# Two all-seeing rounds of the next batch moved to the end of the attention before, in a block-sparse attention with a GELU feed-forward

## The chip, the core and the metric

The kernel runs on one core of one Trainium2 chip. The metric is the device time of one execution in microseconds (us); the time of a kernel is the median over its runs. Engines: TensorE (PE, with its weight loads PEld), VectorE (DVE), ScalarE (ACT), GpSimd (POOL) and SyncE (SP).

## What is computed

The attention is a BigBird pattern: each query block of 32 tokens sees the first and the last key block, its neighbours, itself and three sampled blocks; the first and last query block see every key (these are called all-seeing here). The result, with the heads side by side, goes through a feed-forward layer with an exact GELU.

```python
batch, n_heads, seq, head_dim = (4, 8, 768, 64)
block = 32; n_blocks = 24; n_rand = 3
scores = scale * np.matmul(q, k.transpose(0, 1, 3, 2))
mask = np.abs(blk_i - blk_j) <= 1
mask = mask | (blk_i == 0) | (blk_j == 0) | (blk_i == n_blocks - 1) | (blk_j == n_blocks - 1)
for qb in range(n_blocks):
    for kb in sampled_blocks[qb]:
        mask[qb * block:(qb + 1) * block, kb * block:(kb + 1) * block] = True
scores = np.where(mask, scores, -1000000000.0)
attn = softmax(scores)
x = (attn @ v), heads side by side           # 3072 x 512
h = x @ w_in                                 # 512 -> 2048
out = (0.5 * h * (1.0 + erf(h / sqrt(2)))) @ w_out
```

## The kernel before

**Units.** The 3072 tokens are worked off in nine units. Batch 0 has three (one, two and three quads of 128 tokens), batches 1 to 3 have two each: a *first half* (quads 0 to 2, with the two all-seeing blocks) and a *second half* (quads 3 to 5). For each unit there is an attention, an FFN1 (`ffn1_step`: eight steps of 8 matmuls and a Gelu, writing `g`) and an FFN2 (`ffn2_pieces`: 16 matmuls for each quad, 48 for three quads, 32 for two). The FFN2 of a unit is dealt out, matmul by matmul, into the attention of the unit that follows: it is the `filler`.

**Rounds.** An attention goes in rounds. An ordinary round holds up to two query blocks for all eight heads: scores on PE (`scores`, L301) into one of two PSUM buffers, the negated maxima on DVE (`maxima`, L326), exponentials on ACT (`exponentials`, L338, one instruction for each block and group of heads), a 32x32 transpose on DVE (`turned`, L355). After two rounds the values follow on PE (`values`, L403) in two halves, then a division on DVE (`divided`, L418 to L422), a transpose on PE (`outputs`, L432) and a copy on ACT into `xT` (L437), which FFN1 reads. The all-seeing blocks make four rounds ("d", x, G): x says first or last block, G the group of heads. Their maxima are L329, their transposes go into `ptd` (L359), their values are L379. A first half has these four and six ordinary rounds, a second half six ordinary ones.

**Order.** Nothing reorders the instructions: each engine runs them in the order in which the program issues them. `attention` issues, for each `it`: the scores of round it+1, a division if one is due, the transpose of round it-1, the maxima of round it+1, the exponentials of round it, a finished FFN2 output, hooks, `quota[it + 1]` matmuls of FFN2, an `xT` output, and the values due. The last iteration first takes two FFN2 matmuls. Behind the loop stand the load of ACT's table for Gelu (the one for Exp is loaded in the last step of FFN1) and the `tail`: counts of FFN2 matmuls between the last values, division and output.

**FFN2's output.** One PSUM bank (`psO`, one buffer) collects an output tile. After 16 matmuls, `store_finished` copies it on ACT into `os` (L459; three buffers) and SP stores it (L461). It is called after the exponentials of an iteration, after its FFN2 matmuls unless `late` is set, and before the first matmul of the next output.

**Keys and queries of the next batch.** They are loaded by POOL (`load_by_token`, L111, six transfers for keys and six for queries) in FFN1 of a first half, after `hold_loads(0)`, a one-element copy that waits for FFN1's first Gelu. `turn` (L117, L118) has SP transpose them by DMA into `kTd` (the same memory as `ptd`) and into `qTs`; it is a hook at `it` = 2 of the second half's attention. `place_keys` and `spare_key` (L122, L236) copy the keys, scaled, to their places on DVE; this is done in FFN1 of the second half. There DVE also gathers the keys and values of the blocks seen (`gather_fixed`, `gather`: L249 to L265).

Of the kernel before, what the change touches and what calls it, by code (L numbers as in the profile page):

```python
# [19 lines left out]
def kernel(  # L20
# [121 lines left out]
            out=w_out_sb[:, w * part:w * part + w, :],  # L142
            in_=moe_w_out[P * w * part:P * w * (part + 1)].rearrange("(ko p) f -> p ko f", p=P))

    def hold_loads(m):

        nc.gpsimd.tensor_copy(mark, g[0:1, m, 0:1])  # L147

    def ones(i):
        for hh in range(4):  # L150
# [84 lines left out]
    def spare_key(kT):  # L235
        nc.vector.tensor_copy(kT[:, NB, :], kT[:, 0, :])  # L236
# [23 lines left out]
    def gather(unit, js, at, c0=0, c1=BW, engine=None):  # L260

        src = k0 if (unit.b, c1) == (0, KC) else kvs[unit.b % 2][:, :, c0:c1]
        for j in js:
            for r in range(NR):
                (engine or nc.vector).tensor_copy(sampled(unit.place[j], r)[:, None, c0:c1],  # L265
                                                  src[:, bass.ds(at[j][r], 1), :])


    class Unit:
        def __init__(self, b, quads, dense, i0=0):  # L270
            self.b, self.quads, self.dense = b, quads, dense
            self.groups = [[j for j in range(4 * t, 4 * t + 4) if 0 < j < NB - 1] for t in quads]
            self.js = [j for grp in self.groups for j in grp]
            self.place = {j: i for i, j in enumerate(self.js, i0)}
            self.rounds = [("d", x, G) for x in (0, 1) for G in (0, 1)] if dense else []
            self.ends = {3: tuple(self.rounds)} if dense else {}
            for grp in self.groups:
                r = [("s", tuple(grp[i:i + 2])) for i in range(0, len(grp), 2)]
                self.rounds += r
                self.ends[len(self.rounds) - 1] = tuple(r)  # L280
# [12 lines left out]
    def scores(unit, rnd):  # L293
        qT, kT = qTs[unit.b % 2], keys(unit.b) if unit is not units[0] else k0
        A = psA.tile([P, 1024], F32, name="sc", tag="A")

        def product(o, G, hh, j, rhs):
            r = (hh % 2) ^ G
            rows = slice(64 * r, 64 * r + 64)
            pr = 2 * G + hh // 2  # L300
            nc.tensor.matmul(o, lhsT=qT[rows, j // 4, pr, BL * (j % 4):BL * (j % 4) + BL],  # L301
                             rhs=rhs(rows, pr), start=True, stop=True)
        if rnd[0] == "s":
            A4 = A.rearrange("p (g j c) -> p g j c", g=2, j=2)
            for i, j in enumerate(rnd[1]):
                x = unit.place[j]
                for hh in range(4):
                    for G in range(2):
                        product(A4[32 * hh:32 * hh + 32, G, i, :].rearrange(
                            "p (a c k) -> p a c k", a=2, k=BL), G, hh, j,  # L310
                            lambda rows, pr: seen_keys(x, rows, pr))
        else:
            _, x, G = rnd
            for c0, c1 in ((0, 512), (512, 768)):
                for hh in range(4):
                    product(A[32 * hh:32 * hh + 32, c0:c1], G, hh, (NB - 1) * x,
                            lambda rows, pr: kT[rows, c0 // BL:c1 // BL, BL * pr:BL * pr + BL])
        st[rnd, "A"] = A
# [137 lines left out]
    def store(n, quad, cols, op):  # L456
# [3 lines left out]
        row = units[n].b * S + quad * P  # L460
        nc.sync.dma_start(out=out[row:row + P, cols], in_=os)  # L461

    finished = []

    def ffn2_pieces(n):
# [26 lines left out]
                                 start=(m == 0), stop=(m == KOUT - 1))  # L492
            store(n, quad, cols, op)

    def attention(unit, filler, quota, tail, held=0, hooks=None, late=False):

        rounds, n, hooks = unit.rounds, len(unit.rounds), hooks or {}
        due = [(max(e + 1 + half, held), grp, half) for e, grp in sorted(unit.ends.items())
               for half in range(2)]
        weighed, given = [], []  # L500

        def fill(m):
            for _ in range(m):
                next(filler, None)

        def weigh():
            _, grp, half = due.pop(0)
            values(unit, grp, half)
            if half:
                weighed.append(grp)  # L510

        def divide():
            divided(weighed[0])
            given.append(weighed.pop(0))
        for it in range(-1, n):
            last = it + 1 == n
            if not last:
                scores(unit, rounds[it + 1])
            else:
                fill(2)  # L520
                while due and due[0][0] <= it:
                    weigh()
            ready = len(given)
            if weighed and not last:
                divide()
            if it >= 1:
                turned(rounds[it - 1])
            if weighed and last:
                divide()
            if not last:  # L530
                maxima(rounds[it + 1])
            if it >= 0:
                exponentials(rounds[it])
            store_finished()
            for f in hooks.get(it, ()):
                f()
            fill(quota[it + 1])
            if not late:
                store_finished()
            if ready:  # L540
                outputs(unit, given.pop(0))
            while not last and due and due[0][0] <= it:
                weigh()
        table(AF.Gelu)
        turned(rounds[n - 1])
        fill(tail[0])
        weigh()
        fill(tail[1])
        weigh()
        assert not due  # L550
        while given:
            outputs(unit, given.pop(0))
        divide()
        fill(tail[2])
        outputs(unit, given.pop(0))
        for _ in filler:
            pass
        store_finished()
# [26 lines left out]
    attention(units[0], iter(()), [0] * 7, (0, 0, 0), 5,  # L585
              {4: [lambda: gather(units[0], units[0].js, known, KC, BW)], 5: [second_values]})

    QUOTAS = {0: ([4, 3, 1, 1, 0], (1, 2, 1)), 1: ([6, 5, 5, 3, 3, 1, 1], (2, 2, 1))}
    for n, unit in enumerate(units):
        nxt = units[n + 1] if n + 1 < len(units) else None  # L590
        b = unit.b
        fresh = nxt is not None and nxt.b != b
        if nxt is not None and not fresh:
            gather_fixed(k0 if n == 0 else keys(b), nxt.place)
            if n == 0:
                known |= block_numbers(J0[:3], DVE)
                gather(nxt, J0[:3], known, 0, KC)
                gather(nxt, J0[:3], known, KC, BW)
            elif n == 1:
                known |= block_numbers(J1[:6], DVE)  # L600
                gather(nxt, J1[:6], known)
                gather(nxt, J1[6:7], block_numbers(J1[6:7], DVE))
            else:
                gather(nxt, J1[:6], known)
                for js in (J1[6:9], J1[9:11]):
                    gather(nxt, js, block_numbers(js, DVE))
        for s in range(KOUT // 2):
            ffn1_step(n, 2 * s)
            if s == 0:
                if n == 0:  # L610
                    hold_loads(0)
                    for h in range(H):
                        load_v(1, h)
                    nc.gpsimd.tensor_copy(kvs[0][:, :, 0:KC], k0)
                    gather(units[2], J1[7:], block_numbers(J1[7:], POOL), engine=nc.gpsimd)
                if n > 0 and not fresh and b + 1 < B:
                    hold_loads(0)
                    load_by_token(kn, k, b + 1)
                    load_by_token(qn, q, b + 1)
                if fresh and b + 2 < B:  # L620
                    hold_loads(0)
                    for h in range(H):
                        load_v(b + 2, h)
                if fresh:
                    others = block_numbers(J0[7:], DVE)
            if s == 7 and nxt is not None:
                table(AF.Exp)
            if fresh and s == 0:
                place_keys(b + 1)
                spare_key(keys(b + 1))  # L630
                gather_fixed(keys(b + 1), nxt.place)
                gather(nxt, J0[:7], known)
                gather(nxt, J0[7:], others)
        filler = ffn2_pieces(n)
        if nxt is None:
            last_output(n)
        elif n in QUOTAS:
            attention(nxt, filler, *QUOTAS[n],
                      hooks={2: [lambda: turn(1)]} if n == 1 else None)
        elif fresh:  # L640
            attention(nxt, filler, [6, 6, 4, 0, 6, 6, 4, 0, 2, 2, 1], (2, 3, 3), late=True)
        else:
            attention(nxt, filler, [8, 8, 5, 5, 6, 2, 1], (2, 3, 5),
                      hooks={2: [lambda: turn(b + 1)]} if b + 1 < B else None)


# [28 lines left out]
```

## Time and profile before

| | us |
|---|---|
| median of 3 runs (319.34 to 320.63) | 319.44 |
| the profiled execution | 320.74 |
| its span, first to last instruction | 319.0 |
| PE busy | 268.3 (84%) |
| DVE busy | 218.5 (68%) |
| ACT busy | 208.4 (65%) |
| POOL busy | 88.7 (28%) |
| from FFN1 to FFN1, the three stages with a second half's attention that is followed by another batch | 27.96, 33.35, 32.42 |
| the last second half, which no batch follows | 31.23 |
| from FFN1 to FFN1, first halves | 37.88, 37.28, 37.34 |

The stages run from the first FFN1 matmul (L451) of a unit to that of the next, as the chain of waits lists them: 56.52, 84.48, 122.36, 155.71, 192.99, 225.41, 262.75 and 293.98 us. A stage so has one FFN1 and the attention of the next unit with the FFN2 in it. The first of them has batch 0's second unit, with two quads, for its FFN1. Engine times add up over stages with different limits; which engine holds a stage is read from the waits in it.

### The profile page before, as it was taken

What the parts mean: (1) busy time and instruction counts of PE and PEld (TensorE: products, weight loads), DVE (VectorE), ACT (ScalarE), POOL (GpSimd) and SP (SyncE); (2) the same over time, 40 slices, a digit from 0 to 9 for tenths busy, and PEclk for the clock granted to TensorE, in tenths of its full rate; (3) what the DMA queues carried; (4) which work ended last, traced back from release to release, by engine and by line L of the source; (5) the groups of instructions that cost most, each with busy time, mean ns of one, the idle gap of its engine ahead of it and who ended that gap; (6) DMA issues with size and microseconds to landing.
All of it is one profiled execution on the core that took longest, in us unless ns stands there. A gap on an engine that the chain in (4) does not pass through costs nothing.

```text
span 319.0 us, 12127 instructions
## 1 busy us (share of the span) xinstructions
PE 268.3 (84%) x5240; PEld 147.7 (46%) x5240; DVE 218.5 (68%) x550; ACT 208.4 (65%) x374; POOL 88.7 (28%) x147
## 2 busy tenths in 40 slices
PE   1656877988898879997998889997998789989995
PEld 0615734744453445544553445444543446444643
DVE  6487774798698768785698768874968967673000
ACT  9665483597568775785568765785577765885621
POOL 8659757570070003920160004910000000000000
PEclk9999987799999999998999999999999999999999
DMA  7999999599499100999097101998000000010001
GB/s 110 146 115 208 207 120 31 64 151 171 117 82 52 38 4 35 107 171 189 36 87 47 36 5 37 127 180 159 36 3 35 35 4 35 1 70 4 33 35 67
DMA packets 90632, 25.43 MB, mean 80 GB/s; under 512 B 81745, under 2 KB 87634, under 8 KB 90578
## 3 DMA queue, kind: packets, MB, share of 16 engines
q0 software_dynamic: 68352, 13.64, 79.4%
q1 hardware_dynamic: 22226, 11.01, 14.7%
q8 instruction: 41, 0.67, 0.9%
q14 instruction: 13, 0.11, 0.1%
HBM read 27.26 MB, written 6.29 MB: 105 GB/s over the span
## 4 chain that ended last, share of the span: by engine, by line
PE 66%; DVE 16%; ACT 7%; DMA 5%; issue 3%; POOL 1%; DVEq 0%; POOLq 0%; ACTq 0%
PE hp L451 28%; PE op L470 18%; PE av L403 10%; DVE xh L422 5%; DVE pT L355 4%; PE sc L301 4%; ACT pp L338 4%; DMA w_in_sb<-in_moe_w_in_dram 3%; DVE nm L326 2%; DMA kv<-in_v_dram 2%; PE av L491 2%; PE op L491 2%; DVE rec L420 2%; PE av L379 2%; ACT xT L437 2%
## 5 line engine op out<-in xcount | busy, mean ns | idle before, releaser
L338 ACT ACTIVATE pp<-sc,nm 128x256 bf16<-128x256 f32 (+1 forms) x192 | 92.0, 594 | 22.0 <-DVE nm L326 17.7
L470 PE MATMUL op<-w_out_sb,g 128*128 128x512 bf16 x336 | 91.4, 387 | 2.3 <-ACT os L459 1.3
L451 PE MATMUL hp<-xT,w_in_sb 128*128 128x384 bf16 (+2 forms) x576 | 88.9, 320 | 3.7 <-ACT xT L437 3.7
L454 ACT ACTIVATE g<-hp 128x768 bf16<-128x768 f32 (+4 forms) x81 | 53.8, 676 | 39.2 <-PE hp L451 39.1
L451 PEld LDWEIGHTS <-w_in_sb 128*128 128x128 bf16 x576 | 57.1, 104 | 35.9 <-issue 6.3
L326 DVE TENSOR_REDUCE nm<-sc 128x4 f32<-128x1024 f32 (+1 forms) x48 | 53.4, 1113 | 7.9 <-PE sc L301 7.4
L265 DVE COPY gb<-kv 128x388 bf16 (+1 forms) x240 | 52.2, 295 | 6.1 <-issue 5.9
L403 PE MATMUL av<-kv,pT 64*32 64x130 bf16 x1760 | 39.9, 231 | 15.7 <-DVE xh L422 8.7
L403 PEld LDWEIGHTS <-pT 64*32 64x32 bf16 x2816 | 30.2, 95 | 39.5 <-DVE xh L422 16.4
L470 PEld LDWEIGHTS <-g 128*128 128x128 bf16 x336 | 27.8, 98 | 34.2 <-issue 12.8
L355 DVE STREAM_TRANSPOSE pT<-pp 128x512 f32<-128x512 f32 (+1 forms) x48 | 31.5, 655 | 7.3 <-ACT pp L338 6.9
L147 POOL COPY mark<-g 1x1 bf16<-1x1 bf16 x6 | 6.0, 1002 | 106.6 <-ACT g L454 106.6
L437 ACT COPY xT<-tx 128x512 bf16<-128x512 bf16 (+1 forms) x24 | 13.2, 551 | 28.1 <-PE tx L432 28.1
L301 PE MATMUL sc<-gb,qT 64*32 64x256 bf16 x704 | 19.7, 279 | 10.1 <-ACT pp L338 9.9
L418 DVE TENSOR_SCALAR den<-av 128x8 f32<-128x8 f32 (+2 forms) x28 | 4.5, 161 | 33.9 <-PE av L403 32.2
L130 POOL DMA_DIRECT2D kv<-in_v_dram x32 | 23.3, 735 | 5.2 <-DMA w_out_sb<-in_moe_w_out_dram 3.8
L301 PEld LDWEIGHTS <-qT 64*32 64x32 bf16 x832 | 10.0, 90 | 30.7 <-issue 23.7
L365 ACT ACT_TABLE_LOAD x17 | 21.8, 1283 | 0.3
L403 PE MATMUL av<-gb,pT 64*32 64x130 bf16 x1056 | 20.9, 234 | 0.9 <-issue 0.9
L329 DVE TENSOR_REDUCE nm<-sc 128x1 f32<-128x768 f32 x16 | 15.3, 955 | 6.0 <-PE sc L301 5.5
L422 DVE TENSOR_TENSOR xh<-av,rec 128x512 bf16<-128x512 f32 (+2 forms) x28 | 18.2, 652 | 1.0
L459 ACT COPY os<-op 128x512 f32<-128x512 f32 (+1 forms) x23 | 13.3, 577 | 6.2 <-PE op L491 4.0
(62 smaller groups left out, 203.5 us busy)
## 6 DMA issues: line engine op xcount, KB each, us to landing
out_dram<-os SPq DMA_DIRECT2D x23, 256.0 KB, 2.1
kv<-in_v_dram POOLq DMA_DIRECT2D x32, 96.0 KB, 8.2
kn<-in_k_dram POOLq DMA_DIRECT2D x18, 128.0 KB, 4.6
qn<-in_q_dram POOLq DMA_DIRECT2D x18, 128.0 KB, 5.3
w_in_sb<-in_moe_w_in_dram POOLq DMA_DIRECT2D x4, 512.0 KB, 12.1
w_out_sb<-in_moe_w_out_dram POOLq DMA_DIRECT2D x4, 512.0 KB, 17.6
kn<-in_k_dram POOLq DMA_DIRECT2D x2, 384.0 KB, 5.6
qn<-in_q_dram POOLq DMA_DIRECT2D x2, 384.0 KB, 7.0
```

The source lines that it names most:

```text
L130: nc.gpsimd.dma_start(out=kvs[b % 2][32 * hh:32 * hh + 32, 0:NB, c0:c0 + D], in_=v[b, h].rearrange("(n p) d -> p n d", p=BL))
L265: (engine or nc.vector).tensor_copy(sampled(unit.place[j], r)[:, None, c0:c1], src[:, bass.ds(at[j][r], 1), :])
L301: nc.tensor.matmul(o, lhsT=qT[rows, j // 4, pr, BL * (j % 4):BL * (j % 4) + BL], rhs=rhs(rows, pr), start=True, stop=True)
L326: nc.vector.tensor_reduce(out=nm[:, 0:2 * n].rearrange("p (g j) -> p g j", g=2), in_=A4[:, :, 0:n, :], op=ALU.max, axis=AX.X, negate=True)
L338: nc.scalar.activation(dst.rearrange("p (c k e) -> p c e k", e=2, k=BL), src.rearrange("p (c e k) -> p c e k", e=2, k=BL), AF.Exp, bias=bias)
L355: nc.vector.transpose(pt[:, 0:w].bitcast(F32), pp[:, 0:w].bitcast(F32))
L365: nc.scalar.activation(junk, zero[0:1, 0:1], func)
L403: nc.tensor.matmul(av[32 * s:32 * s + 32, h, V2 * G:V2 * G + V2], lhsT=pv[rows, c // 2, :, c % 2], rhs=src[rows], start=(c == 0), stop=(c ...
L422: nc.vector.tensor_tensor(xh[rows, :, 0:m * D].rearrange("p h (x d) -> p h x d", d=D), a[:, :, :, 0:D], rec[rows, :, 0:m, None].to_broadca ...
L451: nc.tensor.matmul(hp[:, i, 0:T], lhsT=w_in_sb[:, ki, (m + i) * P:(m + i + 1) * P], rhs=xTs[n % 2][:, ki, 0:T], start=(ki == 0), stop=(ki ...
L454: nc.scalar.activation(g[:, m + i[0]:m + i[1], 0:T], hp[:, i[0]:i[1], 0:T], AF.Gelu)
L470: nc.tensor.matmul(op, lhsT=g[:, m, t * P:(t + 1) * P], rhs=w_out_sb[:, m, :], start=(m == 0), stop=(m == KOUT - 1))
```

## The change

The four all-seeing rounds are put in the order (G, x) in place of (x, G). The first two, both of the first group of heads, of each of the batches 1 to 3 now run as the last two rounds of the attention of the unit before (`ahead`, `AHEAD`), which is a second half; the batch's own attention starts with the third (`begun`). So three second halves have eight rounds in place of six, and three first halves eight in place of ten. The values of the all-seeing blocks stay in the first half. The quotas and tails of FFN2 matmuls are new for all these attentions; the last second half keeps its own.

`hold_loads` takes what it waits for, and now waits for an `xT` piece of the first half's second-last group, ahead of FFN1. The turn is issued right behind the loads, and the keys are placed in a hook at `it` = 3 of the second half's attention, no longer in the FFN1 that follows. In the FFN1 before a second half, the blocks whose numbers still have to be read are gathered first.

```diff
-    def hold_loads(m):
-        nc.gpsimd.tensor_copy(mark, g[0:1, m, 0:1])
+    def hold_loads(x):
+        nc.gpsimd.tensor_copy(mark, x)
...
-            self.rounds = [("d", x, G) for x in (0, 1) for G in (0, 1)] if dense else []
+            self.rounds = [("d", x, G) for G in (0, 1) for x in (0, 1)] if dense else []
...
+    AHEAD = 2
+    begun = {}
...
-    def attention(unit, filler, quota, tail, held=0, hooks=None, late=False):
-        rounds, n, hooks = unit.rounds, len(unit.rounds), hooks or {}
-        due = [(max(e + 1 + half, held), grp, half) for e, grp in sorted(unit.ends.items())
+    def attention(unit, filler, quota, tail, held=0, hooks=None, late=False, ahead=None):
+        done = begun.pop(unit, 0)
+        rounds = [(unit, rnd) for rnd in unit.rounds[done:]]
+        due = [(max(e - done + 1 + half, held), grp, half) for e, grp in sorted(unit.ends.items())
                for half in range(2)]
+        if ahead:
+            begun[ahead] = AHEAD
+            rounds += [(ahead, rnd) for rnd in ahead.rounds[0:AHEAD]]
+        n, hooks = len(rounds), hooks or {}
...
         table(AF.Gelu)
-        turned(rounds[n - 1])
-        fill(tail[0])
-        weigh()
-        fill(tail[1])
-        weigh()
+        turned(rounds[n - 1][1])
+        for m in tail[:-1]:
+            fill(m)
+            weigh()
         assert not due
-        while given:
+        while len(given) > (not weighed):
             outputs(unit, given.pop(0))
-        divide()
-        fill(tail[2])
+        if weighed:
+            divide()
+        fill(tail[-1])
         outputs(unit, given.pop(0))
...
-    QUOTAS = {0: ([4, 3, 1, 1, 0], (1, 2, 1)), 1: ([6, 5, 5, 3, 3, 1, 1], (2, 2, 1))}
+    QUOTAS = {0: ([4, 3, 1, 1, 0], (1, 2, 1)), 1: ([5, 5, 4, 3, 2, 2, 2, 2, 2], (2,))}
+
+    def next_batch(n):
+        if n == 0:
+            return {}
+        b = units[n].b + 1
+        return dict(ahead=units[n + 2], hooks={
+            3: [lambda: place_keys(b), lambda: spare_key(keys(b))]})
...
             elif n == 1:
+                gather(nxt, J1[6:7], block_numbers(J1[6:7], DVE))
                 known |= block_numbers(J1[:6], DVE)
                 gather(nxt, J1[:6], known)
-                gather(nxt, J1[6:7], block_numbers(J1[6:7], DVE))
             else:
-                gather(nxt, J1[:6], known)
                 for js in (J1[6:9], J1[9:11]):
                     gather(nxt, js, block_numbers(js, DVE))
+                gather(nxt, J1[:6], known)
...
                 if n > 0 and not fresh and b + 1 < B:
-                    hold_loads(0)
+                    xT, t0 = column[b, unit.groups[-2][0]]
+                    hold_loads(xT[0:1, 0, t0:t0 + 1])
                     load_by_token(kn, k, b + 1)
                     load_by_token(qn, q, b + 1)
+                    turn(b + 1)
...
             if fresh and s == 0:
-                place_keys(b + 1)
-                spare_key(keys(b + 1))
                 gather_fixed(keys(b + 1), nxt.place)
...
-            attention(nxt, filler, *QUOTAS[n],
-                      hooks={2: [lambda: turn(1)]} if n == 1 else None)
+            attention(nxt, filler, *QUOTAS[n], **next_batch(n))
         elif fresh:
-            attention(nxt, filler, [6, 6, 4, 0, 6, 6, 4, 0, 2, 2, 1], (2, 3, 3), late=True)
-        else:
-            attention(nxt, filler, [8, 8, 5, 5, 6, 2, 1], (2, 3, 5),
-                      hooks={2: [lambda: turn(b + 1)]} if b + 1 < B else None)
+            attention(nxt, filler, [5, 6, 5, 5, 4, 4, 4, 3, 2], (2, 3, 3), late=True)
+        elif b + 1 < B:
+            attention(nxt, filler, [7, 7, 5, 5, 4, 4, 3, 2, 4], (4,), **next_batch(n))
+        else:
+            attention(nxt, filler, [8, 8, 5, 5, 6, 2, 1], (2, 3, 5))
```

More of the change, by code (lines that the diff above doesn't have):

```diff
@@ L517, in attention @@
             if not last:
-                scores(unit, rounds[it + 1])
+                scores(*rounds[it + 1])
             else:
@@ L526, in attention @@
             if it >= 1:
-                turned(rounds[it - 1])
+                turned(rounds[it - 1][1])
             if weighed and last:
@@ L530, in attention @@
             if not last:
-                maxima(rounds[it + 1])
+                maxima(rounds[it + 1][1])
             if it >= 0:
-                exponentials(rounds[it])
+                exponentials(rounds[it][1])
             store_finished()
@@ L610 @@
                 if n == 0:
-                    hold_loads(0)
+                    hold_loads(g[0:1, 0, 0:1])
                     for h in range(H):
@@ L616 @@
                 if n > 0 and not fresh and b + 1 < B:
-                    hold_loads(0)
+                    xT, t0 = column[b, unit.groups[-2][0]]
+                    hold_loads(xT[0:1, 0, t0:t0 + 1])
                     load_by_token(kn, k, b + 1)
                     load_by_token(qn, q, b + 1)
+                    turn(b + 1)
                 if fresh and b + 2 < B:
-                    hold_loads(0)
+                    hold_loads(g[0:1, 0, 0:1])
                     for h in range(H):
```

## The prediction

> **What bounds the kernel now.** I read the chain of waits first, then the busy time by stage, TensorE's waits in a stage, and the timeline of one first and one second half.
>
> ```profile
> PE 66%; DVE 16%; ACT 7%; DMA 5%; issue 3%; POOL 1%; DVEq 0%; POOLq 0%; ACTq 0%
> ```
>
> ```profile
> 166.30:193.00 26.70, 22.55 (x631) 10.82 (x628) 20.88 (x37) 19.98 (x40) 0.00 (x0) 1.00 0.49 30
> 193.00:203.60 10.60, 10.60 (x72) 6.27 (x79) 8.93 (x36) 6.12 (x9) 8.18 (x8) 1.00 0.78 72
> 203.60:225.40 21.80, 18.49 (x500) 8.97 (x492) 14.07 (x24) 15.76 (x34) 4.68 (x6) 1.00 1.33 149
> ```
>
> The chain is TensorE's for two thirds. The three rows are a first half's attention, the FFN1 behind it, and the next second half's attention (columns: length, then busy time of PE, PEld, DVE, ACT, POOL). FFN1 has no idle time on PE; attention has 4.2 us of it in a first half and 3.3 in a second. Only this idle time can be won: the change alters no amount of work. In the first half it is spread thinly over short waits:
>
> ```profile
> PE sc L301 <- ACT pp L338: 1.6, 2, 0.8
> PE av L403 <- DVE xh L422: 0.9, 2, 0.6
> PE av L403 <- DVE pT L355: 0.8, 2, 0.4
> PE hp L451 <- ACT xT L437: 0.5, 1, 0.5
> ```
>
> PE, DVE and ACT hand each round on to one another, so a delay on any of them can reach the end of the stage. Three places of the second half's timeline decide below:
>
> ```profile
> 205.89 1.67 ACT L338 ACTIVATE pp<-sc,nm 128x256 bf16<-128x256 f32 x4
> 207.94 0.59 ACT L459 COPY os<-op 128x512 f32<-128x512 f32 x1 [0.39 <-PE op L470]
> 208.43 3.30 ACT L338 ACTIVATE pp<-sc,nm 128x256 bf16<-128x256 f32 x8
> 208.58 1.24 PE L470 MATMUL op<-w_out_sb,g 128*128 128x512 bf16 x5 [0.33 <-ACT os L459]
> ...
> 216.62 0.41 PE L403 MATMUL av<-kv,pT 64*32 64x130 bf16 x28 [0.38 <-DVE pT L355]
> ...
> 220.89 1.28 ACT L365 ACT_TABLE_LOAD   x1
> ...
> 224.71 1.17 DVE L122 TENSOR_SCALAR kv<-ptd 128x768 bf16<-128x768 bf16 x4 [0.27 <-issue]
> 224.88 0.48 ACT L437 COPY xT<-tx 128x384 bf16<-128x384 bf16 x1 [0.67 <-PE tx L432]
> 225.41 2.76 PE L451 MATMUL hp<-xT,w_in_sb 128*128 128x384 bf16 x16 [0.35 <-ACT xT L437]
> ```
>
> There is one `op` bank, so FFN2's 17th matmul waits until ACT has copied the first 16 out (`os`). Now 8+8 matmuls complete the first output at 207.9, just before the second round's exponentials, and the copy goes ahead of them. The table load for Gelu lies well ahead of the last `xT`. The keys are placed (L122) after the last division, where DVE has nothing urgent.
>
> **The change part by part.** Prices, all from this trace: scores 0.36 on PE (seen-by-all round 0.44); one FFN2 matmul 0.233 (six in 1.40); values 0.52 per half of 4 blocks, 0.41 for 3, 0.81 for the all-seeing ones; maxima 1.19 (0.65 for one block, all-seeing 0.97); transpose 0.69 (0.43; all-seeing 0.57); a division 1.07 from `den` to `xh`; exponentials 1.68 for two blocks, 0.90 for one, 1.10 all-seeing; `os` 0.59, `xT` 0.55, table load with its dummy 1.45; placing keys 1.17+0.19 = 1.36. A hand-over between engines costs 0.05 to 0.15. Each engine goes in its own order. Walking the present kernel so, from the start of FFN1 to the start of the next FFN1, gives 30.99 for the last second half (trace: 262.75 to 293.98, 31.23), 37.71 for a first half (155.71 to 192.99, 37.28) and 27.50 for batch 0's last stage (56.52 to 84.48, 27.96). So the walk is good to 0.5 us a stage; differences are taken walk against walk.
>
> *Second half with two rounds added (three such stages).* Work added: PE 0.88, ACT 2.2, DVE 2x0.97+2x0.57+1.36 = 4.4 us; in the trace DVE is idle 7.7 us there. On the clock of the stage above:
> - The quotas 7, 7, 5 put the 16th matmul behind the third round's scores, 208.4 to 208.6. In ACT's order the copy now stands behind the second round's exponentials (207.71 to 209.39), so it ends at 209.98 and the 17th matmul starts at 210.04, where the trace has 208.58: PE idles 1.40. The fourth scores come at 210.74 (trace 210.20), with 19 FFN2 matmuls done and not 21: 0.54+0.47 = 1.0 us lost.
> - Placing the keys (1.36) moves into DVE's order between the fifth round's maxima (to 214.45) and the first division, which then runs from 215.81, and the fourth round's transpose ends at 217.57. Who waits: the second group's values, 217.63 where the trace has 216.62. From 212.4 to 224.9 DVE has 12.6 us of work, so nothing recovers.
> - The added rounds' maxima and transposes stand before the last divisions: second division to 221.26, third 223.23 to 224.30. The second group's transposed output leaves PE behind four matmuls at 224.2; ACT copies it to 224.94, loads the Gelu table to 226.39, and only then copies the last group to 226.94. FFN1 starts at 227.0; the walk of the present kernel on this clock says 223.98: **+3.0**. The table load that was covered now stands in the chain.
> - In two of the stages PE stood 0.94 and 0.91 us on "issue" (at 146.66 and 217.64). PE has 1.75 us of waiting for DVE near there now, so between 0 and 0.9 of it is covered: I take 0.5. So **+2.5 twice**.
> - Batch 0's stage has 32 FFN2 matmuls and quotas 5, 5, 4, 3. The copy stands behind the third round's exponentials, 73.04 to 73.63, the 17th matmul at 73.69 (trace 71.28); second group's values 79.29 (76.59); FFN1 87.96 against 84.00: **+3.9**.
>
> *First half with two rounds removed (three stages).* PE -0.88, ACT -2.2, DVE -3.1, and placing keys leaves FFN1, where DVE only gathers. On the clock of the stage at 155.71: ACT frees its table at 168.75, two all-seeing rounds end at 170.95, the first blocks' exponentials run 171.73 to 173.41 and the copy, which here comes after them, to 174.00. The 16th matmul was done at 171.8, so PE idles 2.2 (trace: 0.8 at this place, 17th matmul 173.02, now 174.06). Rounds are 2.5 us ahead there on ACT. Then the 33rd matmul falls in an iteration with quota 4 and waits for a copy behind the fourth block round's exponentials (180.82 to 182.50, copy to 183.09): 2.05 us idle. The lead is gone: the fifth exponentials start at 184.18 (walk before: 184.17) and FFN1 at 193.66 (193.42): **+0.2 three times**. Between -1.9 (one such wait off) and +1.0 are possible.
>
> *Loads and turns.* Twelve POOL issues and two SP transposes per batch are unchanged in number. On POOL nothing stands behind them before the next FFN1. On SP the turns now stand ahead of the stage's first store, which asks at 209.98 and gets SP after 5.37+4.30 of issuing, at 214.2 at worst; nothing waits for it, as there are three `os` buffers and the third copy after it comes at 226.9 or later. The hold waits for the second-last `xT` copy (191.65), not for FFN1's first Gelu.
>
> ```profile
> 195.43 2.33 POOL L147 COPY mark<-g 1x1 bf16<-1x1 bf16 x1 [30.75 <-ACT g L454]
> 197.70 5.30 POOL L111 DMA_DIRECT2D kn<-in_k_dram  x6
> 209.19 5.37 SPq L117 DMA_TRANSPOSE ptd<-kn  x1
> 214.79 4.30 SPq L118 DMA_TRANSPOSE qT<-qn  x1
> ```
>
> The hold's copy took 2.33 us beside 18 DVE copies (0.18 at 59.14). Loads start between 191.9 and, if it must wait for DVE's first pause, 194.7. The six key loads take 5.3 and land 4.6 after the last issue: turn issued by 204.5; it lands in 6.2 to 9.0: 213.5 at worst, and DVE asks at 214.45. Queries: 12.9 from the first turn's issue to the second's landing, 217.4, asked at 218.15. So nothing, with 0.7 to 1 us to spare; batch 0's stage has about the same (80.9 at worst against 79.81). The new order of the gathers changes nothing the scores wait for over 0.3 us.
>
> Sum: 3.9+2.5+2.5+3x0.2 = 9.5. Against the profiled execution: span 319.0+9.5 = 328.5, and with the 1.74 around it (320.74) 330.2. That execution was 1.30 above the median of the runs, so on the median 319.44+9.5 = **328.9**.
>
> The Trainium skill, page "SBUF — State Buffer", section on SWDGE ("The DVE blocks DMA trap"), says that loads issued from GpSimd get no descriptors written while VectorE holds the port pair they share, as its fast copies do. The hold's 2.33 us agree; the issues do not: six key loads took 0.88 us each while DVE copied, as the query loads did with DVE mostly free. By that rule the time would be that of the rival of the held loads, below.
>
> **The rivals.**
> - *The first half keeps its lead*: if PE's wait at the 33rd matmul is covered, 1.85 us come back three times: 9.5-5.6 = +3.9, 323.3. For it: the lead of 2.5 us; against: `os` stands behind 1.68 us of exponentials in ACT's order.
> - *Faster: the rounds fill idle time.* The first half loses 0.88 of PE work and the 1.6 of waits for ACT between its first scores, and the second takes 0.88 into its 3.3 idle us: -1.6 a pair, -4.8, 314.6. It decides if the second half is no longer than now plus 0.9. For it: each engine's busy sum leaves room. Against: `os` behind the exponentials and DVE's filled stretch.
> - *Keys and queries late*: if the hold yields no earlier load than now (197.70), turns start at 206.8, keys land at 215.8 and queries at 219.7: 1.5 us late in each of three stages, +4.5, 333.4. For it: the hold's copy met DVE's fast copies before, and does again. Against: DVE pauses at 194.7 for the block numbers, which are now read first.
> - *Loads held until DVE's copies end* (203.4): key loads landed at 212.4, turned at 221.4, 7.0 us after DVE asks; three times, +21 on top of the sum, 350. Against: key loads at 0.88 us each beside DVE's copies.
> - *It cancels*: the first halves gain what the second ones lose (3.0 a pair, against the 1.85 and 1.6 above), within 1.6 us of now.
>
> **How the numbers follow.** Forecast 0.68; first half ahead 0.10; late loads 0.08; loads held 0.01; faster 0.09; cancelled 0.04. 0.5% (1.6 us) is about what a measurement here can tell from no change. Slower: 0.68+0.10+0.08+0.01 = 0.87; same 0.04; faster 0.09. Range: the forecast's own is 325 to 332 (0.5 us of error in each of six stages); reaching into the neighbours on both sides, 322 to 333.
>
> **What would show it.** Right: ACT `os` behind exponentials and PE idle 1 to 2 us before the 17th FFN2 matmul in all six stages; DVE L122 between maxima and `den` in the middle of a second half; a table load just before its last `xT`; second halves from FFN1 to FFN1 of 34 and more, first halves near 37.5. Wrong: second halves under 33, or first halves under 36; DVE waiting for a DMA at L122 would show the late loads.

## The result, and the profile after

| | before | after |
|---|---|---|
| median, us (range, runs) | 320.03 (319.34 to 321.88, 4) | 333.11 (332.18 to 333.51, 4) |
| span of the profiled execution | 319.0 | 331.7 |
| FFN1 to FFN1, batch 0's last unit | 27.96 | 35.22 |
| second halves of batches 1 and 2 | 33.35, 32.42 | 34.78, 35.01 |
| last second half (no batch follows) | 31.23 | 31.23 |
| first halves of batches 1, 2 and 3 | 37.88, 37.28, 37.34 | 37.98, 37.90, 39.39 |
| the stage ahead of these, from batch 0's first FFN1 | 22.64 | 21.30 |

The ratio is 1.0395 (95% interval 1.0343 to 1.0448): slower. Of the span's 12.7 us, 7.26 lie in batch 0's last unit, 1.43 and 2.59 in the two second halves, 0.10, 0.62 and 2.05 in the first halves; the stage ahead, whose code is the same, gave 1.34 back. In it the granted clock was 0.57 from 52 to 58 us before, and 0.61 after, but 0.72 against 1.00 from 46 to 52. The ratios leave out the few executions that took over 1.5% longer than the fastest of their kernel, the medians do not.

PE's part of the chain of waits of the kernel after fell from 66% to 43%; DVE's rose from 16% to 24% and ACT's from 7% to 13% (DVEq, ACTq and POOLq are the sequencers of these engines; "issue" is time in which an engine waited for nothing that the profile shows):

```profile
PE 43%; DVE 24%; ACT 13%; DMA 8%; issue 7%; DVEq 3%; POOL 1%; ACTq 0%; POOLq 0%
```

Part of PE's fall is the path: in the FFN1 of two first halves the chain now runs through DVE's gathers (127.26 to 140.9 and 199.90 to 213.9 us) and no longer through 10.56 us of matmuls. PE's waits name the place of the loss. These are rows of the kernel before, whose FFN2 is L470, and of the kernel after (total, times, longest):

```profile
PE op L470 <- ACT os L459: 1.3, 4, 0.3
...
PE op L473 <- ACT os L459: 15.5, 10, 2.1
PE av L403 <- DVE xh L422: 12.1, 13, 3.6
PE sc L301 <- ACT pp L338: 8.1, 9, 1.6
PE op L473 <- issue: 8.0, 48, 0.3
```

The last of these rows should not be read as a loss: the trace after has only 269 records of the FFN2 matmuls, the one before has 336 of the same number, and a gap stands where a record is missing.

The timeline of the kernel after, in the second half of batch 2 (start, length; in brackets the idle time before and what ended it):

```profile
218.15 0.63 ACT L459 COPY os<-op 128x512 f32<-128x512 f32 x1
...
218.82 0.59 PE L473 MATMUL op<-w_out_sb,g 128*128 128x512 bf16 x2 [1.05 <-ACT os L459]
...
223.23 1.16 DVE L122 TENSOR_SCALAR kv<-ptd 128x768 bf16<-128x768 bf16 x4
...
233.56 0.59 ACT L437 COPY xT<-tx 128x512 bf16<-128x512 bf16 x1 [0.96 <-PE tx L432]
...
234.16 1.28 ACT L365 ACT_TABLE_LOAD   x1
...
235.56 0.45 ACT L437 COPY xT<-tx 128x384 bf16<-128x384 bf16 x1
...
236.07 1.14 PE L451 MATMUL hp<-xT,w_in_sb 128*128 128x384 bf16 x6 [1.29 <-ACT xT L437]
```

Three of the signs that the prediction names are there: PE stands before the 17th FFN2 matmul until ACT has copied, the keys are placed in mid-attention, and the table load now separates the last two `xT` copies, so that FFN1 starts 1.29 us after PE was free.

In the first half of batch 2 PE waits twice, before the 17th and before the 33rd matmul:

```profile
181.12 1.24 PE L473 MATMUL op<-w_out_sb,g 128*128 128x512 bf16 x4 [2.10 <-ACT os L459]
...
189.92 0.38 PE L473 MATMUL op<-w_out_sb,g 128*128 128x512 bf16 x1 [1.75 <-ACT os L459]
```

In the last first half, the copy stands behind 1.72 us of exponentials:

```profile
251.84 1.72 ACT L338 ACTIVATE pp<-sc,nm 128x256 bf16<-128x256 f32 x4 [0.82 <-DVE nm L326]
...
253.39 0.60 ACT L459 COPY os<-op 128x512 f32<-128x512 f32 x1
...
254.04 1.71 PE L473 MATMUL op<-w_out_sb,g 128*128 128x512 bf16 x4 [2.11 <-ACT os L459]
...
255.68 1.51 PE L379 MATMUL av<-kv,ptd 64*64 64x130 bf16 x48
```

and the busy time there by stretches of 2 us (after the x-counts of PE, PEld, DVE, ACT and POOL come the granted clock, the DMA share and GB/s) shows what came behind the wait:

```profile
252.00:254.00 2.00, 0.00 (x0) 0.00 (x0) 1.27 (x3) 2.00 (x6) 0.00 (x0) 1.00 0.00 0
254.00:256.00 2.00, 1.91 (x16) 0.76 (x20) 0.30 (x1) 0.83 (x2) 0.00 (x0) 0.67 0.34 131
256.00:258.00 2.00, 1.75 (x60) 1.23 (x54) 0.18 (x1) 0.00 (x0) 0.00 (x0) 0.50 0.04 8
```

After 2 us without a matmul the clock fell to half; the 48 all-seeing value matmuls took 1.51 us, and 0.88 at full clock (258.83). In the first half of batch 2 the same wait, the 2.10 us above, left the clock at 1.00.

Batch 0's last unit is the one place where the keys came late in this kernel:

```profile
50.34 6.51 POOL L265 COPY gb<-kv 128x388 bf16 x12
...
56.92 5.42 POOL L111 DMA_DIRECT2D kn<-in_k_dram  x6
...
66.89 5.91 SPq L117 DMA_TRANSPOSE ptd<-kn  x1
...
76.90 1.17 DVE L122 TENSOR_SCALAR kv<-ptd 128x768 bf16<-128x768 bf16 x4 [1.78 <-DMA ptd<-kn]
...
79.39 0.24 PE L403 MATMUL av<-kv,pT 64*32 64x130 bf16 x4 [3.62 <-DVE xh L422]
```

POOL gathers for batch 0 until 56.85, so the loads could not start sooner; the turn took 10.0 us from its issue to its landing. DVE stood 1.78 us on it with everything behind it, PE 3.62, and the clock behind that wait was 0.65 from 80 to 82 and 0.50 from 82 to 84.

### The profile page after: what moved, and what is told of

The parts are those of the page before. It is cut to its first block, busy times and chain, and to the rows that moved or that the text cites. A ratio compares the mean times of both kernels' runs of the same rounds, so it can differ in the third digit from the quotient of the medians.

```text
span 331.7 us, 12047 instructions
## 1 busy us (share of the span) xinstructions
PE 255.0 (77%) x5172; PEld 146.4 (44%) x5240; DVE 216.5 (65%) x550; ACT 208.3 (63%) x374; POOL 93.5 (28%) x147
## 4 chain that ended last, share of the span: by engine, by line
PE 43%; DVE 24%; ACT 13%; DMA 8%; issue 7%; DVEq 3%; POOL 1%; ACTq 0%; POOLq 0%
PE hp L451 19%; PE op L473 8%; PE av L403 8%; ACT pp L338 7%; DVE xh L422 5%; DVE gb L265 4%; DVE nm L326 4%; DVE pT L355 4%; DMA ptd<-kn 3%; DMA w_in_sb<-in_moe_w_in_dram 3%; DMA kv<-in_v_dram 2%; ACT L365 2%; DVEq L205 2%; PE av L379 2%; PE av L494 2%
## 5 line engine op out<-in xcount | busy, mean ns | idle before, releaser
L473 PE MATMUL op<-w_out_sb,g 128*128 128x512 bf16 x269 | 76.6, 384 | 24.3 <-ACT os L459 15.5
L451 PEld LDWEIGHTS <-w_in_sb 128*128 128x128 bf16 x576 | 56.1, 102 | 39.7 <-issue 9.3
L326 DVE TENSOR_REDUCE nm<-sc 128x4 f32<-128x1024 f32 (+1 forms) x48 | 53.2, 1114 | 12.8 <-PE sc L301 12.4
L265 DVE COPY gb<-kv 128x388 bf16 (+1 forms) x240 | 50.4, 289 | 9.3 <-issue 8.9
L403 PE MATMUL av<-kv,pT 64*32 64x130 bf16 x1760 | 37.9, 226 | 19.5 <-DVE xh L422 12.1
L403 PEld LDWEIGHTS <-pT 64*32 64x32 bf16 x2816 | 28.8, 93 | 41.5 <-DVE xh L422 19.2
L473 PEld LDWEIGHTS <-g 128*128 128x128 bf16 x336 | 26.6, 98 | 41.8 <-issue 21.0
L437 ACT COPY xT<-tx 128x512 bf16<-128x512 bf16 (+1 forms) x24 | 13.1, 548 | 19.7 <-PE tx L432 19.7
L147 POOL COPY mark<-g 1x1 bf16<-1x1 bf16 x3 | 8.5, 2843 | 53.4 <-ACT g L454 53.4
L301 PEld LDWEIGHTS <-qT 64*32 64x32 bf16 x832 | 11.3, 91 | 24.5 <-issue 20.5
L403 PE MATMUL av<-gb,pT 64*32 64x130 bf16 x1056 | 20.0, 228 | 0.0
L111 POOL DMA_DIRECT2D kn<-in_k_dram x18 | 17.0, 961 | 0.3 <-issue 0.3
```

Source lines behind the costliest of these rows:

```text
L326: nc.vector.tensor_reduce(out=nm[:, 0:2 * n].rearrange("p (g j) -> p g j", g=2), in_=A4[:, :, 0:n, :], op=ALU.max, axis=AX.X, negate=True)
L403: nc.tensor.matmul(av[32 * s:32 * s + 32, h, V2 * G:V2 * G + V2], lhsT=pv[rows, c // 2, :, c % 2], rhs=src[rows], start=(c == 0), stop=(c ...
L451: nc.tensor.matmul(hp[:, i, 0:T], lhsT=w_in_sb[:, ki, (m + i) * P:(m + i + 1) * P], rhs=xTs[n % 2][:, ki, 0:T], start=(ki == 0), stop=(ki ...
L473: nc.tensor.matmul(op, lhsT=g[:, m, t * P:(t + 1) * P], rhs=w_out_sb[:, m, :], start=(m == 0), stop=(m == KOUT - 1))
```

## The experiments

Times are medians; each ratio is to the kernel before, run on the same chip (319.67, 319.58 and 319.54 us in the three groups), with its 95% interval. Stages are those of the table, from the profiled execution.

**The moves alone.** The first run is the kernel before with the early hold, turn and new order of gathers; the second is the changed kernel with no round ahead and the old quotas, so that the placing of the keys (and the order of the all-seeing rounds) is added to the first.

```diff
-                    hold_loads(0)
+                    xT, t0 = column[b, unit.groups[-2][0]]
+                    hold_loads(xT[0:1, 0, t0:t0 + 1])
...
+                    turn(b + 1)
```

> The kernel before with one part alone: the earlier hold, the turn right behind the loads, and the new order of the gathers; no rounds are moved, quotas and place of the keys as before. Theory A (FFN2's copies behind exponentials, DVE's filled order and the table load carry the loss; the loads add only what DVE's gathers are slowed by while POOL issues): the gathers end about 2 us later in the FFN1 before each of three second halves, the first maxima about 1.4 us later, so +2 to +4 us on 320. Theory B (the loads and turns carry the loss): +8 us or more. Theory C (loads cost nothing): within 1 us.

```diff
-    AHEAD = 2
+    AHEAD = 0
...
-            attention(nxt, filler, [5, 6, 5, 5, 4, 4, 4, 3, 2], (2, 3, 3), late=True)
+            attention(nxt, filler, [6, 6, 4, 0, 6, 6, 4, 0, 2, 2, 1], (2, 3, 3), late=True)
...
-            attention(nxt, filler, [7, 7, 5, 5, 4, 4, 3, 2, 4], (4,), **next_batch(n))
+            attention(nxt, filler, [8, 8, 5, 5, 6, 2, 1], (2, 3, 5), **next_batch(n))
```

> The changed kernel with no round moved ahead (AHEAD = 0) and the quotas and tails of before; the early loads and the placing of the keys in the middle of the second half stay. Theory A: the loads' part as in the run with the loads alone, and 1.0 us for each of three placings of 1.36 us in DVE's order, less what the first halves' FFN1 gains (nothing): +5 to +7 us on 320. In batch 0's last stage DVE waits for the keys as it did in the changed kernel (1.8 us). Theory B (the moved rounds carry the loss): within 2 us of before.

Measured: 320.66 us, 1.0024 (1.0000 to 1.0048), and 321.92 us, 1.0061 (1.0036 to 1.0087). Both expectations were too high: 2 to 4 us for the first run, 5 to 7 for the second. Loads, turns, gathers and placing together cost about 2 us of the 13 (2.8 at the end of the interval); the rest is the rounds with their quotas. Loads are not free where they run. This is the timeline of the first of the two runs, in FFN1 of a first and of a second half:

```profile
192.35 5.68 POOL L111 DMA_DIRECT2D kn<-in_k_dram  x6
...
197.20 8.58 DVE L265 COPY gb<-kv 128x388 bf16 x33 [2.32 <-issue]
197.97 5.36 POOL L111 DMA_DIRECT2D qn<-in_q_dram  x6
...
228.19 5.70 DVE L265 COPY gb<-kv 128x388 bf16 x33
```

33 gathers took 0.26 us each while POOL issued loads and 0.173 each without. The kernel before has both in one FFN1, as its loads started at 197.70: 0.174 us each ahead of them and 0.29 beside them.

```profile
194.57 3.14 DVE L265 COPY gb<-kv 128x388 bf16 x18
...
199.07 4.35 DVE L265 COPY gb<-kv 128x388 bf16 x15 [1.35 <-issue]
```

The second half of batch 2 was no longer for the earlier loads (31.79 against 32.42), since a wait of 0.91 us on "issue" had gone; that of batch 1 was 33.89 against 33.35. Batch 0's stage was 28.53 and, with the keys placed in mid-attention, 31.47; there DVE stood 0.99 us on the keys, PE 2.95, and the clock was 0.64 from 78 to 82.

**The quotas.** All rounds stay ahead; only the numbers of FFN2 matmuls are chosen so that the 16th, 32nd matmul come just ahead of a round's exponentials. The first run changes all three attentions, the second the first halves alone (`late` goes in both); the third only takes `late` off there, so that the copy is issued right behind the matmuls that complete an output and no longer behind the next exponentials.

```diff
-    ... 1: ([5, 5, 4, 3, 2, 2, 2, 2, 2], (2,))}
+    ... 1: ([6, 5, 5, 3, 3, 1, 1, 3, 1], (2,))}
...
-            attention(nxt, filler, [5, 6, 5, 5, 4, 4, 4, 3, 2], (2, 3, 3), late=True)
+            attention(nxt, filler, [6, 7, 3, 4, 1, 5, 6, 2, 5], (3, 0, 4))
...
-            attention(nxt, filler, [7, 7, 5, 5, 4, 4, 3, 2, 4], (4,), **next_batch(n))
+            attention(nxt, filler, [8, 8, 5, 5, 6, 3, 2, 3, 1], (4,), **next_batch(n))
```

> The changed kernel with other quotas and tails alone: the 16th FFN2 matmul ends an iteration, so that its copy goes ahead of the next exponentials, in second halves (8, 8, 5, 5, 6, 3, 2, 3, 1), batch 0 (6, 5, 5, 3, 3, 1, 1, 3, 1) and first halves (6, 7, 3, 4, 1, 5, 6, 2, 5; tail 3, 0, 4; copy right after the matmuls). Theory A: first halves from 37.9-39.4 to 33 to 35 us from FFN1 to FFN1, second halves 1 us shorter each: 12 to 18 us less than the changed kernel, 315 to 321. Theory B (the quotas don't matter, DVE's work does): 331 to 334.

The second: the middle edit alone.

> The changed kernel with the new quotas in the three first halves alone (6, 7, 3, 4, 1, 5, 6, 2, 5; tail 3, 0, 4; copy right after the matmuls); second halves keep the quotas of the change. Theory A (the copies behind exponentials cost most where two of them meet, in the first halves): first halves 33.4 to 36.4 us from FFN1 to FFN1 as in the run with all new quotas, 10 to 12 us less than the changed kernel, 321 to 323. Rival (it takes both quotas, since the half that is shortened waits for the other): under 5 us, over 328.

```diff
-            attention(nxt, filler, [5, 6, 5, 5, 4, 4, 4, 3, 2], (2, 3, 3), late=True)
+            attention(nxt, filler, [5, 6, 5, 5, 4, 4, 4, 3, 2], (2, 3, 3))
```

> The changed kernel with one word off: the first halves' FFN2 output is copied right after the 16th matmul's iteration and not behind the next exponentials (late off); all quotas stay. Theory A (the copy's place in ACT's order): the wait of 2.1 us ahead of the 17th matmul is gone in three first halves, the one ahead of the 33rd (1.75) stays; the same walk as in the prediction gives 1.8 less each, so 5 to 6 us less than the changed kernel, and the fall of the clock in the last first half goes with the wait: 325 to 328. Rival (how the matmuls are dealt out matters, not the copy): 331 to 334.

| | us | ratio (95%) | first halves | second halves | batch 0 |
|---|---|---|---|---|---|
| after | 333.11 | 1.0395 (1.0343 to 1.0448) | 37.98, 37.90, 39.39 | 34.78, 35.01 | 35.22 |
| `late` removed | 327.07 | 1.0214 (1.0148 to 1.0280) | 36.23, 36.22, 36.24 | 34.91, 35.24 | 34.53 |
| first halves' quotas | 319.44 | 0.9996 (0.9950 to 1.0043) | 34.63, 33.96, 33.37 | 34.70, 34.42 | 33.74 |
| all quotas | 316.03 | 0.9872 (0.9839 to 0.9906) | 36.36, 34.40, 33.37 | 33.36, 32.85 | 31.96 |

For the first halves the one word shows that the copy's place is a cause, worth 6 us of the 13. This is the last first half with `late` removed, where the copy goes ahead of the exponentials:

```profile
249.63 0.59 ACT L459 COPY os<-op 128x512 f32<-128x512 f32 x1 [0.72 <-PE op L473]
...
250.11 2.52 ACT L338 ACTIVATE pp<-sc,nm 128x256 bf16<-128x256 f32 x6
...
250.26 1.24 PE L473 MATMUL op<-w_out_sb,g 128*128 128x512 bf16 x4 [0.44 <-ACT os L459]
```

and PE's waits with all quotas changed:

```profile
PE op L473 <- ACT os L459: 2.3, 6, 0.4
```

PE waits 0.44 us at this place in place of 2.11, its clock stays at 1.00, and the stage is 3.15 us shorter; the other two first halves lose 1.75 and 1.68. With the quotas the row falls from 15.5 us to 2.3. The quotas of the first halves alone (with their tail and without `late`) take away the whole loss, 0.9996 against 1.0395, with the second halves still about as long as in the changed kernel: a first half with two rounds less and the new quotas is 3.3 to 4.0 us shorter than before (37.88, 37.28, 37.34). How much of that is the rounds is not shown, since no run gave the kernel before, with all its rounds in place, a new deal of FFN2.

**The table load.** Behind an attention with rounds ahead, it is issued after the last `xT` copy.

```diff
-        table(AF.Gelu)
+        if not ahead:
+            table(AF.Gelu)
...
+        if ahead:
+            table(AF.Gelu)
```

> The changed kernel with the Gelu table loaded behind the last copy into xT in the three second halves with rounds ahead. Theory A: the table load of 1.45 us leaves the chain there, as the first Gelu comes 1.5 us behind FFN1's start anyway: 1.0 to 1.3 us less in each, 3 to 4 us less than the changed kernel, 329 to 330. Rival: the first Gelu is late by as much and FFN1, with two PSUM buffers, waits for it: no difference.

The changed kernel with this edit, at the end of the second half of batch 2:

```profile
232.35 0.48 ACT L437 COPY xT<-tx 128x384 bf16<-128x384 bf16 x1 [0.45 <-PE tx L432]
232.85 1.28 ACT L365 ACT_TABLE_LOAD   x1
232.88 7.39 PE L451 MATMUL hp<-xT,w_in_sb 128*128 128x384 bf16 x44 [0.35 <-ACT xT L437]
```

Measured: 330.96 us, 1.0354 (1.0289 to 1.0419); the three stages are 1.52, 0.90 and 0.99 us shorter, FFN1 waits 0.35 us and the load lies beside its matmuls. The first figure does not measure the table load, since the keys came in time in batch 0's stage here. The interval overlaps that of the changed kernel; what shows the effect is the wait in the trace, and the run with quotas and table edit below. The last first half was again long here (39.46), with a wait of 2.10 before its 17th matmul and a lowered clock.

**No rounds for batch 1.** Quotas as above, and batch 0's last unit does no rounds ahead and places no keys; batch 1's first half has its ten rounds and the quotas of before.

```diff
-        if n == 0:
+        if n <= 1:
             return {}
...
+                if n == 2:
+                    place_keys(b + 1)
+                    spare_key(keys(b + 1))
```

> The kernel with all new quotas, but no rounds of batch 1 ahead: batch 0's last stage and batch 1's first half go as before the change (keys placed in FFN1, 10 rounds, quotas of before). Theory A (in batch 0's last stage the keys come late, since POOL is still gathering for batch 0, and TensorE's clock falls in the wait): that stage from 32.0 back to about 28.3, batch 1's first half from 36.4 to 37.3: 2.5 to 3 us less than the run with all new quotas, 313 to 314. Rival (the clock falls there whatever the keys do): no less than 315.5.

Measured: 316.52 us, 0.9915 (0.9876 to 0.9954), no better than with all rounds ahead. The expectation failed in batch 0's stage: it was 31.88, though its code is that of the run of the early loads, where it was 28.53. With the same code it was 29.89 in the last run below. The granted clock goes along with it: 1.00 throughout in the run of 28.53, 0.65 from 70 to 74 us in that of 29.89, and 0.64 there with 0.72 and 0.86 from 78 to 86 in that of 31.88. Nothing here settles why it falls in one and not in another.

**Loads still earlier.** Quotas and table load as above, and the hold waits for the first `xT` copy of the first half, so that the key loads of batch 3 start 11.1 us ahead of FFN1 and not 1.7; once with all rounds ahead, once without those of batch 1.

```diff
-                    xT, t0 = column[b, unit.groups[-2][0]]
+                    xT, t0 = column[b, 0]
```

> The kernel with all new quotas, the Gelu table behind the last copy into xT where rounds are ahead, and the loads held for the first copy into xT of the first half (the all-seeing blocks') in place of the second-last. Theory A: the table gives 1.0 to 1.5 us three times; the loads of batches 2 and 3 then run beside the attention, where DVE has few fast copies, so its gathers take 5.7 to 6 us and not 8.6 and end before FFN1 does: 0 to 0.6 us twice. 310 to 313. Rival (loads beside the attention take from it what the gathers gain): 313 and more.

> The kernel without rounds of batch 1 ahead and with new quotas, and with the table load and the hold of the run beside it. Theory A: both together: 308 to 311.5. Rival as for the run beside it: 312 and more.

Measured: 320.36 us, 0.9987 (0.9945 to 1.0029), and 322.87, 1.0086 (1.0051 to 1.0121). Both expectations failed (310 to 313 and 308 to 311.5), and both kernels are slower than those with the same quotas without this and without the table edit (316.03 and 316.52). So the last two runs have the quotas and the table edit only, with all rounds ahead and without those of batch 1:

> The kernel with all new quotas, with the Gelu table behind the last copy into xT where rounds are ahead; the hold stays as in the change. Theory A: 1.0 to 1.3 us less in each of three second halves than with the quotas alone, 312 to 313.5. If the earlier hold, not the table, made the two kernels with both slow, this one shows it. Rival (the table moved is what made them slow): 316 and more.

> The kernel with new quotas and no rounds of batch 1 ahead, with the Gelu table behind the last copy into xT in the two second halves with rounds ahead; the hold as in the change. Theory A: 2.0 to 2.6 us less than without the table's move, 314. Batch 0's last stage, which the same kernel took 31.9 us for with a wait on issue and a lower clock, and the kernel with the loads alone 28.5, shows once more whether that comes and goes.

Measured: **313.26 us**, 0.9777 (0.9717 to 0.9836), and 314.87, 0.9814 (0.9742 to 0.9886). The first has the lowest median here, 2.2% under the kernel before; their intervals overlap, so the two are not told apart. In the first run the first halves take 34.73, 34.52 and 33.43 us, the second halves 32.42 and 32.05, batch 0's last unit 31.52, which is still 3.6 more than before. The table edit gives about 1% on top of the quotas (0.9872 without it). The pairs with and without the earlier hold differ in that one line, by 2.1% and 2.7% of the time before. The view of waits has, without it (no rounds for batch 1),

```profile
DVE gb L265 <- issue: 11.9, 7, 2.3
...
PE tx L432 <- issue: 1.3, 6, 0.5
```

and with it

```profile
DVE gb L265 <- issue: 19.1, 9, 5.0
...
PE av L403 <- issue: 3.9, 5, 1.7
PE tx L432 <- issue: 3.5, 6, 2.7
...
196.17 0.50 PE L432 MATMUL tx<-identity,xh 128*128 128x128 bf16 x3 [2.71 <-issue]
```

The loads now run beside the end of the first half's attention, and there PE and DVE stand for nothing that the profile shows: 2.71 us at 196.17, before an `xT` transpose, with the clock at 0.50 from 196 to 202. What holds them was not tried and stays open.

## Why the prediction was right, and where it was not

**Slower, by the mechanism named.** Forecast +9.5 us, measured +13.1 on the medians (+12.7 on the spans). The median, 333.11, lies at the range's upper end, 333; the ratio times the median shown then gives 332.1. That the sum came so near is in part luck: batch 0's stage was 3.4 us longer than forecast and the last first half 1.9, while a second half was 1.1 shorter and the stage ahead gave back 1.3.

**Second halves, +2.5 twice:** +1.43 and +2.59, with lengths of 34.78 and 35.01. The 17th matmul waited 1.05 where 1.40 was worked out. PE's waits on "issue" in these stages were gone, so the whole 0.9 us was covered where 0.5 was taken: 3.0-0.9 = 2.1, and the mean measured is 2.0. The table load in the chain was right: 0.90 and 0.99 us come back without it. That these stages stay at 34.4 to 35.2 when only the first halves are mended shows that the loss is theirs.

**First halves, +0.2 three times:** +0.10 and +0.62, as walked: 2.5 us of lead lost again in two waits behind exponentials. One wait less was priced at 2.1 us (from +0.2 to -1.9); the one word won 1.75 and 1.68. The third, +2.05, failed: the walk had PE's 2.2 us of idleness and priced the work behind it at full clock. By an estimate from the granted clock, the two stretches at 0.67 and 0.50 cost up to 2x0.33+2x0.50 = 1.7 us.

**Batch 0's last unit, +3.9:** +7.26. Two steps failed. The first is "batch 0's stage has about the same" spare: the figures behind that sentence, 80.9 at worst against 79.81, already say 1.1 us too late. The turn was issued at 66.89 and took 10.0 us, where 6.2 to 9.0 were assumed, and DVE waited 1.78. The second is that everything was priced at one clock. The late keys do not explain most of it. The runs with the first halves' quotas and without `late` have this stage's code unchanged, and in both DVE did not wait for the keys at L122 (with the quotas the queries came 0.52 us late). This is PE's wait without `late`, where the changed kernel has 3.62:

```profile
79.44 0.24 PE L403 MATMUL av<-kv,pT 64*32 64x130 bf16 x4 [1.75 <-DVE xh L422]
```

Yet the stages took 33.74 and 34.53 us, +5.8 and +6.6 over the kernel before, and the clock fell all the same (0.50 and 0.72 from 80 to 84 in the one, 0.76 and 0.50 in the other). These stages are 1.5 and 0.7 us shorter than with late keys, one execution each, and 1.9 and 2.7 us beyond the forecast came without late keys. In the changed kernel a mean clock of 0.57 from 80 to 84 is by an estimate up to 1.7 us of PE's time. A slow FFN1 need not count: its 64 matmuls took 9.55 us (8.68 before), but without `late` they took 7.18, and PE then stood 3.17 us for exponentials. No run took the clock apart from the waits, and why it falls there stays open. In other stages the keys were in time, and the rival of the late keys, which wanted 1.5 us in each of three stages, holds for one.

**The gathers, nothing over 0.3 us:** for the scores this holds, but in the second half of batch 2 the gathers ended at 213.89, 12.8 us after FFN1's start, where the kernel before had 10.4 (203.42 from 193.00). DVE's first maxima, behind them, came 1.8 us later in the stage and ACT waited 1.02 for them. The early loads alone had the same delay (the gathers ended 12.8 us after FFN1's start), and their two second halves were 0.54 longer and 0.63 shorter than before, so it was not the main cause.

**The other rivals.** Loads held until DVE's copies end: no, six key loads were issued in 5.75 us beside them. The page "SBUF — State Buffer" of the Trainium skill, section "Who interferes with whom", says that VectorE in its fast copies and GpSimd lock each other out of one port pair; the trace agrees only in that the gathers took 0.26 in place of 0.173 us each, not that the loads stood. First half ahead by 1.85 us: not in the changed kernel; removing `late` gives nearly as much (1.75 and 1.68), but by the other wait, the one at the 17th matmul. Faster, because the rounds fill idle time: its condition, second halves no longer than before plus 0.9, failed in the changed kernel and is met in the fastest one (32.42 and 32.05), where the gain is larger than the -1.6 a pair said. So the rounds ahead need not cost time; the quotas given with them did.

## What to carry to other kernels

Where one PSUM bank collects an output, the copy that frees it belongs in the walk: find in ScalarE's order what stands ahead of it at every 16th matmul, for one iteration too late cost 2.1 us here. When work is moved between stages, deal out the filler anew for both; the same move was 4% slower or 2% faster by the quotas, `late` and the place of one table load. A transfer moved ahead is to be judged by what runs beside it: sooner was not better once it met the end of the attention.

## What the hardware did that was not expected

- The clock fell to 0.50 behind a wait of PE of 2.11 us and stayed at 1.00 behind one of 2.10 in the first half before it; with the table load moved it fell to 0.50 behind one of 2.10 too. So the length of the one wait does not decide here, and what does stays open. It fell too behind 3.62 us (0.65, then 0.50). The Trainium skill, page "TensorE: Matmul & The Clock Gate", "Part 1: The HAM clock gate", gives an idle window of about 3.4 us; the shorter wait that was followed by half rate differs from it, and the measurement decides.
- While POOL issued loads, DVE's small copies took 1.5 times as long (0.26 against 0.173 us; in the kernel before 0.29 against 0.174). That they go together in these stretches is shown; how POOL slows DVE was not tried.
- The same DMA transpose landed 10.0 us after its issue, where the kernel before shows 6.2 to 9.0.
